# Running sums turned to rows by TensorE, new buffer rule and new order in a scheduled attention and two-MLP kernel

## The chip, the cores and the metric

The kernel runs on 1 core of a Trainium2 chip. Its time is device microseconds of one execution; the runs before the change took 653.19 to 654.08 us, median 653.97 us of 3. Besides, one execution was recorded by the hardware profiler. Engines: PE is TensorE's matmul, PEld its weight load, DVE is VectorE, ACT ScalarE, POOL GpSimd, SP SyncE, which here issues all loads and stores.

## The reference

Attention for 4 batches of 8 heads, 576 tokens, head width 64, with a bias from running sums of s; then two MLP blocks over all 2304 tokens. Cut to what matters:

```python
scores = q @ k.T / sqrt(64)
cum = cumsum(maximum(s, 0), axis=-1)
bias = -(cum[:, None] - cum[None, :])            # per head
scores = where(causal, -1e9, scores + minimum(bias, 0))
attn = softmax(scores)                           # sum + 1e-9
x = (attn @ v)                                   # heads side by side: 2304 x 512
h = x @ w_in; e = exp(h - max(h)); u = h * e / sum(e)
ln = (u - mean(u)) / sqrt(var(u) + 1e-6) * g_ln  # 1024 wide
x2 = ln @ w_out                                  # back to 512
out = maximum(maximum(x2 @ w1, x2 @ w2), x2 @ w3) @ w_out2
```

## The kernel before

**Work.** Two batches form a pair p (c = 0, 1 names the batch in it). A pair has nine tiles t of 128 tokens: for j = 0 to 3 one tile of each batch, and a last one with the 64 left-over tokens of both. Per tile: `prep` loads k, q and v and turns k and q (for the first tiles by TensorE, `turned`, later by a transposing DMA), `scores` multiplies, `half` masks, exponentiates and turns the result, `values` multiplies with v, `m1` does the first MLP's input side. Tiles go two by two into nine groups; per group `m2` multiplies with w_out, `m3` with w1, w2, w3 and takes the maxima (L1257), `m4` with w_out2. Nearly all values are split into a high and a low 16-bit part, and each product is three matmuls of parts.

**Weights.** Each of 40 weight pieces of 512 columns arrives as a 64-bit pattern in one of four staging buffers (the second halves of `kt` and `vs`, not yet needed) and is decoded by `load_w`: three VectorE instructions (L654, L660, L663), a ScalarE copy to the high part (L668), and the low part either by TensorE and ScalarE (L672, L675) or by one more VectorE instruction (L678).

**The bias.** The running sums `cum` of s are put into the scores by a product of their own (L854): `ckr` holds for each head three 16-bit parts of the sums beside rows of ones, `cq` the same for the queries. Batch c and the head's parity y own rows 32c + 64y up. `prologue` computes the sums with heads on partitions (L578 relu, L580 scan, L589 and L588 split in three), writes them to DRAM as `cum_d` (L591), and `load_c` and `load_cq` read them back turned into rows (L603, L616). The first tile's scores need ckr and cq of its pair.

**The order.** `build` writes each operation down with its possible engines, an estimated length and a position `pos`; `Schedule.run` plans them with those estimates: at each step an engine takes among the operations that could start soon (`look`) the one with the smallest pos plus its unit's entry in `off`. The result fixes the order on each engine and the buffer that each operation gets; the semaphores follow from it. The numbers in `P` thus set the order. After the plan is written, an engine works its list in order and waits where an operand is not there. Some loads are held back by hand (L1313 and L1319: the loads of k for tile 1, of v for tile 0, of g and of some weights are issued after the sums' loads).

## Time and profile before

| | |
|---|---|
| median of 3 runs | 653.97 us (653.19 to 654.08) |
| profiled execution | 653.85 us, its span 652.1 us |
| busy: PE, DVE, ACT, POOL | 608.0, 451.4, 328.4, 5.1 us |
| HBM read | 35.95 MB |

The span runs from the first to the last instruction of the program; what the execution takes beside it lies around it. Busy time is the union of an engine's instructions; matmuls overlap, so a busy TensorE is not at its peak. A wait names the engine or DMA whose event came last.

### The profile page before, as it was taken

The numbers are of one execution on the slowest core, as the hardware profiler recorded it, in microseconds if no ns is written. First come the engines' busy times: TensorE is split into PE (matmuls) and PEld (weight loads), VectorE is DVE, ScalarE is ACT, GpSimd is POOL, SyncE is SP. The second block draws the span as 40 slices with busy tenths as digits, with TensorE's granted clock in tenths as the row PEclk, the third lists the DMA queues.
The fourth block names the chain that finished last, engine by engine and source line by source line (L and its number), as shares of the span: only waits on it lengthen the run. The fifth ranks groups of instructions, "written<-read, shape, count | busy, mean of one in ns | idle before, by whom it ended". The sixth has DMA issues, their size and how long they took to land.

```text
span 652.1 us, 15319 instructions
## 1 busy us (share of the span) xinstructions
PE 608.0 (93%) x6203; PEld 447.2 (69%) x6203; DVE 451.4 (69%) x1083; ACT 328.4 (50%) x767; POOL 5.1 (1%) x18
## 2 busy tenths in 40 slices
PE   3386888899999999999999999999999999999997
PEld 1154546785777778778687678677777777777884
DVE  7489999999598659663878676585858576526031
ACT  4378987358565547563644444473446455303100
POOL 3000000000000000000000000000000000000000
PEclk9999899999999999999999999999999999999999
DMA  6579675687999657838769685765374456421001
GB/s 174 172 224 250 169 183 171 193 155 135 180 142 169 146 118 124 150 52 174 123 121 185 134 166 94 131 121 91 73 137 92 93 89 106 82 50 33 33 1 32
DMA packets 249830, 82.67 MB, mean 127 GB/s; under 512 B 226048, under 2 KB 244576, under 8 KB 249760
## 3 DMA queue, kind: packets, MB, share of 16 engines
q1 hardware_dynamic: 249760, 81.70, 61.5%
q8 instruction: 48, 0.79, 0.5%
q14 instruction: 22, 0.18, 0.1%
HBM read 35.95 MB, written 4.83 MB: 63 GB/s over the span
## 4 chain that ended last, share of the span: by engine, by line
PE 81%; DVE 11%; DMA 3%; issue 2%; ACT 2%; SPq 1%; DVEq 0%
PE acc L1238 31%; PE acc L1199 13%; PE w L1102 12%; PE acc L1272 11%; PE w L860 4%; PE av L1029 3%; DVE acc L660 3%; PE w L854 2%; DVE acc L663 2%; PE av L1016 2%; PE acc L486 1%; DVE f L654 1%; DVE w_h L678 1%; DMA kt<-in_moe_w_in_dram 1%; DMA et<-es 1%
## 5 line engine op out<-in xcount | busy, mean ns | idle before, releaser
L1238 PE MATMUL acc<-x2A,w_h 128*128 128x256 f16 x1296 | 214.4, 273 | 2.2 <-DVE f L1257 1.5
L1238 PEld LDWEIGHTS <-w_h 128*128 128x128 f16 x1944 | 188.0, 98 | 27.8 <-issue 4.0
L1238 PE MATMUL acc<-x2B,w_h 128*128 128x256 f16 x648 | 176.8, 273 | 0.0
L945 ACT ACTIVATE r<-r,mn 128x128 f32<-128x128 f32 (+4 forms) x144 | 83.0, 578 | 52.2 <-DVE mn L892 42.0
L1102 PE MATMUL w<-w_in_h,xt 128*128 128x512 f16 x432 | 100.2, 381 | 0.3 <-ACT xt L503 0.3
L1199 PE MATMUL acc<-lnt,w_out_h 128*128 128x256 f16 x864 | 98.6, 273 | 0.4 <-ACT lnt L503 0.4
L1199 PEld LDWEIGHTS <-w_out_h 128*128 128x128 f16 x864 | 83.4, 98 | 13.3 <-issue 1.5
L446 DVE SCALAR_TENSOR_TENSOR es<-r,es 128x512 f16<-128x512 f32 (+1 forms) x92 | 58.2, 638 | 24.0 <-ACT es L417 23.8
L1102 PEld LDWEIGHTS <-xt 128*128 128x128 f16 x432 | 41.6, 98 | 47.4 <-issue 2.6
L1257 DVE TENSOR_TENSOR f<-f,acc 128x512 f32<-128x512 f32 x54 | 37.0, 686 | 45.6 <-PE acc L1238 45.3
L892 DVE CUSTOM_DVE_ANT_0 r<-w,mask 128x128 f32<-128x128 f32 (+3 forms) x128 | 58.3, 487 | 9.8 <-PE w L860 8.4
L1272 PE MATMUL acc<-w2o_h,h2A 128*128 128x512 f16 x216 | 64.5, 380 | 0.0
L417 ACT ACTIVATE es<-r 128x512 f16<-128x512 f32 (+1 forms) x73 | 42.8, 592 | 40.5 <-DMA et<-es 34.8
L466 ACT ACTIVATE f<-acc 128x512 f32<-128x512 f32 x37 | 22.0, 595 | 81.7 <-PE acc L1238 49.7
L860 PE MATMUL w<-kt,qt 64*128 64x256 f16 (+2 forms) x768 | 45.0, 262 | 0.0
L1116 DVE TENSOR_SCALAR_CACHE_REDUCE e<-w 128x1024 f32<-128x1024 f32 x18 | 22.0, 1223 | 31.7 <-PE w L1102 31.7
L1029 PEld LDWEIGHTS <-et 128*128 128x128 f16 x960 | 35.0, 99 | 9.8 <-issue 2.6
L1272 PE MATMUL acc<-w2o_h,h2B 128*128 128x512 f16 x108 | 41.0, 380 | 0.0
L1029 PE MATMUL av<-vs,et 128*128 128x64 f16 x960 | 37.6, 195 | 1.1 <-ACT et L503 0.6
L860 PEld LDWEIGHTS <-qt 64*128 64x128 f16 (+1 forms) x864 | 33.9, 102 | 5.8 <-issue 1.3
L854 PE MATMUL w<-ckr,cq 64*128 64x128 bf16 (+5 forms) x192 | 25.7, 308 | 12.0 <-DMA ckr<-cum_d 11.2
L1272 PEld LDWEIGHTS <-h2A 128*128 128x128 f16 x216 | 19.5, 98 | 21.1 <-issue 2.0
(132 smaller groups left out, 688.4 us busy)
## 6 DMA issues: line engine op xcount, KB each, us to landing
kt<-in_moe_w_dram SPq DMA_DIRECT2D x18, 256.0 KB
vs<-in_moe_w_dram SPq DMA_DIRECT2D x18, 256.0 KB
raw<-in_k_dram SPq DMA_DIRECT2D x16, 256.0 KB
raw<-in_q_dram SPq DMA_DIRECT2D x16, 256.0 KB
raw<-in_v_dram SPq DMA_DIRECT2D x16, 256.0 KB
out_dram<-f SPq DMA_DIRECT2D x16, 256.0 KB
kt<-in_moe_w_out_dram SPq DMA_DIRECT2D x7, 512.0 KB
vs<-in_moe_w_out_dram SPq DMA_DIRECT2D x7, 512.0 KB
```

The costliest lines, as they stand in the source:

```text
L417: eng.activation(out=out(g), in_=src(g), func=AF.Copy, scale=sc(g))
L446: nc.vector.scalar_tensor_tensor(out=lo(g), in0=src(g), scalar=sc1(g), in1=hi(g), op0=ALU.mult, op1=ALU.subtract)
L854: yield lambda: nc.tensor.matmul(out=out(), lhsT=T["cq"][i][r, hp, 0:ts.stop - ts.start], rhs=T["ckr"][r, hp, ck], start=True, stop=False, ...
L860: yield lambda n=n, qa=qa, o=o, kx=kx: nc.tensor.matmul(out=out()[:, o], lhsT=qv()[r, qa * HP + hp, ts], rhs=kx, start=False, stop=(n == 2 ...
L892: nc.vector.tensor_tensor_reduce(out=gw(R)[:, g], in0=gw(sc[y])[:, g], in1=T["mask"][:, SM - W:SM], scale=1.0 / S_MUL, scalar=3e38, op0=AL ...
L945: nc.scalar.activation(out=gw()[:, g], in_=gw()[:, g], func=AF.Exp, bias=mnf()[:, g:g + 1], scale=-1.0, accum_out=den(hs[g]),)
L1029: nc.tensor.matmul(out=out, lhsT=ea_[:, ea, kb], rhs=T["v_s"][c, kb // 2][:, kb % 2, ha + a, va], start=(kb == 0 and m == 0), stop=(kb == ...
L1102: nc.tensor.matmul(out=hb()[:, n * 512:(n + 1) * 512], lhsT=xt()[:, xa, kk], rhs=T["w_in_h"][:, wa, kk, n * 512:(n + 1) * 512], start=(kk ...
L1199: nc.tensor.matmul(out=ps()[:, d % 2 * GN:(d % 2 + 1) * GN], lhsT=T["w_out_h"][:, wa, kk, d * 128:(d + 1) * 128], rhs=lnt()[:, la, kk], st ...
L1238: nc.tensor.matmul(out=ps()[:, f % 2 * GN:(f % 2 + 1) * GN], lhsT=T["w123_h"][:, w, wa, f, kk], rhs=x2(xa)[:, kk], start=(kk == 0 and i == ...
L1257: op([("DVE", dve2(2 * GN), lambda ps=ps: nc.vector.tensor_tensor(out=m(), in0=m(), in1=ps(), op=ALU.max))], pk + [m], [m], pos, kind="m3x")
L1272: nc.tensor.matmul(out=ps(), lhsT=h2(ha)[:, f, o * 128:(o + 1) * 128], rhs=T["w2o_h"][:, wa, f], start=(f == 0 and i == 0), stop=(f == KF2 ...
```

## The change

The sums are computed in two pieces, columns 0 to 127 first (relu, scan, split), then the rest. `first_sums` multiplies the first piece with `pick`, a matrix of zeros and ones that sends heads to the rows of ckr and cq, 24 matmuls in two buffers of PSUM; ScalarE or VectorE copies the results to ckr's first 128 columns and to cq, with signs and ones from `rows`. The sums still go to DRAM; ckr's other 448 columns, and cq from tile 2 on, come from there. The scores of tiles over 128 columns wait for the second key `ckB`. For batch 0 the bias product reads 33 rows, not 64, and does not wait for batch 1's. g is loaded as 8 rows of 128 and turned by one matmul. The loads held back by hand behind the sums' loads are no longer so.

The planner's rules: an operation whose buffer another has begun is planned no earlier than that buffer's release (`since`), no more than eight transfers are open at once, and estimates of some lengths differ. P's numbers, `off` with several hundred entries above all, set another order on every engine.

```diff
--- before.py
+++ after.py
...
-    la=5.521,
...
+    la=-6.043,
...
-    off={},
+    off={
+        "c": -52.41, "c.": -55.92, "c0.": -56.71, "c1.": -57.46, "h0.0": -17.18, "h0.2": -32.17,
...
+                    at = max(at, b.since)
...
+                lanes = lanes[1:] + [o.end]
+                free[e] = max(free[e], lanes[0])
...
+                    h = b.pool.holder[b.slot]
+                    b.since = h.end + self.LAT_CROSS if h else 0
...
+    def first_sums(c3, cb, pos):
+        for n in range(2):
+            wb = buf("w")
+            def f(n=n, wb=wb):
+                for x in range(HP):
+                    for i in range(3):
+                        m = 3 * n + 3 - i
+                        nc.tensor.matmul(
+                            out=wb()[:, x * 128:(x + 1) * 128], lhsT=T["pick"][0:BH, x, m:m + 128], rhs=c3()[:, i, 0:128],
+                            start=(i == 0), stop=(i == 2), skip_group_check=True,
+                        )
+            op([("PE", pe(12, 128) + 100, f)], [(cb, 0), "pick"], [wb], pos + n, kind="cs")
+            ps = lambda wb=wb: wb()[:, 0:HP * 128].rearrange("p (x t) -> p x t", t=128)
+            for c in range(2) if n else (None,):
+                def f_a(c=c, ps=ps):
+                    nc.scalar.activation(
+                        out=T["ckr"][:, :, 0:128] if c is None else T["cq"][c], in_=ps(), func=AF.Identity,
+                        scale=1.0 if c is None else T["rows"][:, c:c + 1], bias=T["rows"][:, 2 if c is None else 3 + c:][:, 0:1])
+                def f_v(c=c, ps=ps):
+                    if c is None:
+                        nc.vector.tensor_scalar(out=T["ckr"][:, :, 0:128], in0=ps(), scalar1=T["rows"][:, 2:3], scalar2=None, op0=ALU.add)
+                    else:
+                        nc.vector.tensor_scalar(
+                            out=T["cq"][c], in0=ps(), scalar1=T["rows"][:, c:c + 1], scalar2=T["rows"][:, 3 + c:4 + c],
+                            op0=ALU.mult, op1=ALU.add)
+                op([("ACT", act(512, True, False, True), f_a), ("DVE", dve2(512) + 61, f_v)], [wb, "rows"],
+                   [("ck", x, y) for x in range(2) for y in range(2)] if c is None else [("cq", c, y) for y in range(2)],
+                   pos + n + (c or 0) / 4, kind="ce")
...
-            op([("POOL", 400, lambda c=c: nc.gpsimd.memset(T["cq"][c].bitcast(F32), 0.0))],
-               [], [("cq", c, y) for y in range(2)], p0, kind="one")
...
+        op([("POOL", 330, lambda: nc.gpsimd.memset(T["pick"], 0.0))], [], ["pick"], p0 - 0.9, kind="one")
+        op([("DVE", 90, lambda: nc.vector.tensor_copy(
+            T["pick"][:, :, 6:6 + 128].rearrange("p x (y c r) -> p x y c r", y=2, c=2)[:, :, :, :, 0],
+            IDENT()[0:BH, 0:2 * H].rearrange("p (c x y) -> p x y c", c=2, y=2)))], ["ktail", "pick"], ["pick"], p0 - 0.9, kind="one")
...
+        for n, (lo, hi) in enumerate(((0, 128), (128, S))):
+            w = hi - lo
+            op([("ACT", act(w) + 60, lambda lo=lo, hi=hi: nc.scalar.activation(
+                out=spt()[:, lo:hi], in_=spt()[:, lo:hi], func=AF.Relu, scale=S_MUL))],
+               [sp], [(sp, n)], p0 + n / 2, kind="relu0")
+            def scan(lo=lo, hi=hi):
+                nc.vector.tensor_tensor_scan(
+                    out=cmt()[:, lo:hi], data0=spt()[:, lo:hi], data1=spt()[:, lo:hi],
+                    initial=cmt()[:, lo - 1:lo] if lo else 0.0, op0=ALU.add, op1=ALU.max)
+            op([("DVE", w * 1.71 + 300, scan)], [(sp, n)] + [(cum, 0)] * n, [(cum, n)], p0 + n / 2, kind="scan")
+            def parts(lo=lo, hi=hi):
+                sl, cl = spt()[:, lo:hi], cmt()[:, lo:hi]
+                for i in range(3):
+                    src = cl if i == 0 else sl
+                    if i:
+                        nc.vector.tensor_tensor(out=sl, in0=cl if i == 1 else sl, in1=c3()[:, i - 1, lo:hi], op=ALU.subtract)
+                    nc.vector.tensor_copy(c3()[:, i, lo:hi], src)
+            op([("DVE", 2450 if n else 1900, parts)], [(cum, n), (sp, n)], [(sp, n), (cb, n)], p0 + n / 2 + 0.1, kind="c3")
+            if n == 0:
+                first_sums(c3, cb, p0 + 0.2)
...
+                op([("SP", 450, lambda c=c, y=y, r0=r0: nc.sync.dma_start(out=T["ckr"][r0:r0 + 3, :, lo:S], in_=cd[2 * p + c, y][:, :, lo:S]))],
+                   ["cum_d", "ck1"], [("ck", c, y)] * (p > 0) + [("ckB", c, y)], pos, dma=300, kind="c")
+            if p:
+                load_cq(t + c, pos)
...
-            out=T["g_sb"], in_=X["g_ln"].rearrange("(k p) -> p k", p=128), single_packet=False))],
-            [], ["g0"], P["wo"] - 0.5, dma=448, kind="g")
+            out=T["g_raw"], in_=X["g_ln"].rearrange("(k p) -> k p", p=128)))],
+            [], ["g0"], P["wo"] - 0.5, dma=30, kind="g")
+        gp = buf("w")
+        op([("PE", 200, lambda: nc.tensor.matmul(
+            out=gp()[:, 0:KF], lhsT=T["g_raw"], rhs=IDENT()[0:KF, 0:KF], is_transpose=True, start=True, stop=True,
+            skip_group_check=True))], ["g0", "ktail", "prime"], [gp], P["wo"] - 0.5, kind="gp")
         op([("DVE", 73, lambda: nc.vector.tensor_scalar(
-            out=T["g_sb"], in0=T["g_sb"], scalar1=W_S, scalar2=None, op0=ALU.mult))], ["g0"], ["g"], P["wo"] - 0.5, kind="gs")
+            out=T["g_sb"], in0=gp()[:, 0:KF], scalar1=W_S, scalar2=None, op0=ALU.mult))], [gp], ["g"], P["wo"] - 0.5, kind="gs")
...
-        keyed = [(x, i, y) for x in ("ck", "cq") for i in ((0, 1) if tail else (c,)) for y in range(2)]
+        both = (0, 1) if tail or c else (0,)
+        keyed = [("cq", i, y) for i in ((0, 1) if tail else (c,)) for y in range(2)] + [
+            (x, i, y) for x in ("ck", "ckB")[:1 + (W > 128)] for i in both for y in range(2)]
...
+            rb = slice(64 * y, 64 * y + (64 if i else 33))
-                out=out(), lhsT=T["cq"][i][r, hp, 0:ts.stop - ts.start], rhs=T["ckr"][r, hp, ck], start=True, stop=False,
+                out=out(), lhsT=T["cq"][i][rb, hp, 0:ts.stop - ts.start], rhs=T["ckr"][rb, hp, ck], start=True, stop=False,
...
-    for k, n in (("ldk1", "cum"), ("ldv0", "c00"), ("ldq1", "c00"), ("g", "c00")):
-        named[k].after.add(named[n])
...
```

TensorE, first scores. The order of before from the copies of q on (`qt` is q's transposed tile, `acc` and `w` are buffers in PSUM):

```order
L500 MATMUL acc_130<-qt_89,k_tail 128x512
L672 LDWEIGHTS k_tail
L672 MATMUL acc_131<-w_in_h,k_tail 128x512
L672 LDWEIGHTS k_tail
L672 MATMUL acc_129<-w_in_h,k_tail 128x512
L854 LDWEIGHTS cq_79
L854 MATMUL w_126<-ckr,cq_79 128x128
```

The same place after (`lnt_112` holds the split sums):

```order
L591 MATMUL acc_133<-qt_92,k_tail 128x512
L628 LDWEIGHTS pick
L628 MATMUL w_130<-lnt_112,pick 128x128
...
L628 MATMUL w_129<-lnt_112,pick 128x128
L1008 LDWEIGHTS cq_79
L1008 MATMUL w_130<-ckr,cq_79 128x128
```

Two weight products (L672) stood ahead of the first scores; now the 24 products with pick stand there, and no weight product.

VectorE, from the split of the sums to the first mask-add (ISA with `mask`), before (`f` holds a decoded half, `kt` and `vs` are the staging buffers):

```order
L589 CAST lnt_109<-ln_108 32x576
L654 TENSOR_SCALAR f_115<-kt_69 128x512
...
L663 SCALAR_TENSOR_TENSOR acc_130<-kt_69,acc_130 128x512
L654 TENSOR_SCALAR f_115<-vs_73 128x512
L660 SCALAR_TENSOR_TENSOR acc_131<-vs_73,f_115 128x512
L663 SCALAR_TENSOR_TENSOR acc_131<-vs_73,acc_131 128x512
L697 TENSOR_SCALAR g_sb<-g_sb 128x8
L892 ISA r_91,mn_118<-w_126,mask 128x128
```

And after:

```order
L733 CAST lnt_112<-ln_111 32x448
L801 TENSOR_SCALAR f_118<-kt_69 128x512
L801 TENSOR_SCALAR f_119<-vs_73 128x512
L807 SCALAR_TENSOR_TENSOR acc_134<-kt_69,f_118 128x512
L807 SCALAR_TENSOR_TENSOR acc_132<-vs_73,f_119 128x512
L810 SCALAR_TENSOR_TENSOR acc_134<-kt_69,acc_134 128x512
L810 SCALAR_TENSOR_TENSOR acc_132<-vs_73,acc_132 128x512
L801 TENSOR_SCALAR f_120<-kt_71 128x512
L1046 ISA r_94,mn_121<-w_130,mask 128x128
```

Four pieces are decoded ahead of the first mask-add before, two pieces and the first step of a third now.

VectorE, last decode and group 1's `x2B` (the low part of m2's result), before:

```order
L663 SCALAR_TENSOR_TENSOR acc_131<-vs_75,acc_131 128x512
L446 SCALAR_TENSOR_TENSOR es_94<-r_92,es_94 128x384
L1128 ISA e_107,st_125<-e_107,ln_108 128x1024
...
L446 SCALAR_TENSOR_TENSOR xs_106<-f_116,xs_106 128x512
L1216 SCALAR_TENSOR_TENSOR x2B_112<-acc_129,x2A_111 128x512
```

And after:

```order
L1370 SCALAR_TENSOR_TENSOR x2B_115<-acc_132,x2A_114 128x512
L1046 ISA r_96,mn_123<-w_130,mask 128x384
...
L825 SCALAR_TENSOR_TENSOR w2o_h<-acc_134,w2o_h 128x512
L801 TENSOR_SCALAR f_119<-vs_75 128x512
L807 SCALAR_TENSOR_TENSOR acc_132<-vs_75,f_119 128x512
L537 SCALAR_TENSOR_TENSOR es_97<-r_94,es_97 128x384
L810 SCALAR_TENSOR_TENSOR acc_132<-vs_75,acc_132 128x512
...
L1370 SCALAR_TENSOR_TENSOR x2B_115<-acc_133,x2A_114 128x512
```

Before, group 1's first x2B stands 39 rows behind the last decode (L663). Now it stands ahead of the last decode (L810), and the second x2B seven rows behind that.

## Rows read from the trace of the kernel before

**Rows 1.** The page, busy us, share of the span and instructions.

```profile
PE 608.0 (93%) x6203; PEld 447.2 (69%) x6203; DVE 451.4 (69%) x1083; ACT 328.4 (50%) x767; POOL 5.1 (1%) x18
```

**Rows 2.** The page, the chain that ended last, by engine.

```profile
PE 81%; DVE 11%; DMA 3%; issue 2%; ACT 2%; SPq 1%; DVEq 0%
```

**Rows 3.** Busy time in stretches: length; PE, PEld, DVE, ACT, POOL; PEclk, DMA, GB/s.

```profile
0.00:150.00 150.00, 112.16 (x907) 74.00 (x907) 132.08 (x313) 96.61 (x226) 5.13 (x18) 0.99 0.70 186
150.00:200.00 50.00, 48.85 (x538) 36.16 (x537) 40.47 (x100) 34.45 (x81) 0.00 (x0) 1.00 0.94 160
200.00:500.00 300.00, 300.00 (x3218) 223.31 (x3216) 208.25 (x511) 153.28 (x367) 0.00 (x0) 1.00 0.68 125
...
27.20:151.00 123.80, 105.16 (x875) 70.42 (x874) 119.53 (x291) 89.79 (x217) 0.00 (x0) 0.99 0.70 182
```

**Rows 4.** TensorE's waits over the whole span: us in total, times, longest.

```profile
PE w L854 <- DMA ckr<-cum_d: 11.2, 2, 10.1
```

**Rows 5.** VectorE's waits in the first 30 us, same columns.

```profile
DVE r L892 <- PE w L860: 8.1, 1, 8.1
DVE f L654 <- DMA kt<-in_moe_w_in_dram: 2.7, 2, 1.9
...
DVE f L654 <- DMA vs<-in_moe_w_in_dram: 0.7, 1, 0.7
```

**Rows 6.** SyncE's queue in order of time: start, length in us, what.

```profile
0.80 0.41 SPq L534 DMA_DIRECT2D ln<-in_s_dram  x1
```

**Rows 7.** TensorE in order of time, the first scores.

```profile
25.23 0.26 PE L854 MATMUL w<-ckr,cq 64*128 64x128 bf16 x1 [1.18 <-DMA ckr<-cum_d]
...
25.53 0.39 PE L854 MATMUL w<-ckr,cq 64*128 64x128 bf16 x2
...
25.96 0.39 PE L854 MATMUL w<-ckr,cq 64*128 64x128 bf16 x2
```

**Rows 8.** VectorE in order of time, five places.

```profile
5.42 0.75 DVE L588 TENSOR_TENSOR ln<-e,lnt 32x576 f32<-32x576 f32 x1
...
6.69 0.75 DVE L588 TENSOR_TENSOR ln<-ln,lnt 32x576 f32<-32x576 f32 x1
...
8.64 0.43 DVE L654 TENSOR_SCALAR f<-kt 128x512 int32<-128x512 int32 x1 [0.72 <-DMA kt<-in_moe_w_in_dram]
...
27.25 0.29 DVE L892 CUSTOM_DVE_ANT_0 r<-w,mask 128x128 f32<-128x128 f32 x1 [8.13 <-PE w L860]
...
151.52 0.70 DVE L663 SCALAR_TENSOR_TENSOR acc<-vs,acc 128x512 int32<-128x512 int32 x1
```

**Rows 9.** ScalarE in order of time, two places.

```profile
2.85 0.68 ACT L578 ACTIVATE ln<-ln 32x576 f32<-32x576 f32 x1 [0.77 <-DMA ln<-in_s_dram]
...
8.18 0.60 ACT L503 ACTIVATE qt<-acc 128x512 f16<-128x512 f32 x1 [0.18 <-PE acc L500]
```

**Rows 10.** VectorE by line and shape: busy us, mean ns of one, idle before.

```profile
L663 DVE SCALAR_TENSOR_TENSOR acc<-kt,acc 128x512 int32<-128x512 int32 x20 | 13.8, 690 | 0.2
...
L654 DVE TENSOR_SCALAR f<-kt 128x512 int32<-128x512 int32 x20 | 8.3, 417 | 2.7 <-DMA kt<-in_moe_w_in_dram 2.7
...
L580 DVE TENSOR_TENSOR_SCAN e<-ln 32x576 f32<-32x576 f32 x1 | 1.3, 1345 | 0.3 <-ACT ln L578 0.3
...
L589 DVE CAST lnt<-ln 32x576 bf16<-32x576 f32 x2 | 0.9, 447 | 0.1
```

**Rows 11.** SyncE's queue, the last issues.

```profile
648.15 1.18 SPq L1285 DMA_DIRECT2D out_dram<-f  x2
```

**Rows 12.** POOL in order of time, two places.

```profile
1.08 0.65 POOL L542 TENSOR_SCALAR_AFFINE_SELECT k_tail<-k_tail 128x128 f32<-128x128 f32 x2
...
5.03 1.25 POOL L574 TENSOR_SCALAR_AFFINE_SELECT maskt<-maskt 64x64 bf16<-64x64 bf16 x2
```

**Rows 13.** TensorE by line and shape, two groups of 256 columns.

```profile
L1238 PE MATMUL acc<-x2A,w_h 128*128 128x256 f16 x1296 | 214.4, 273 | 2.2 <-DVE f L1257 1.5 <-ACT f L466 0.7
...
L860 PE MATMUL w<-kt,qt 64*128 64x256 f16 x384 | 30.1, 269 | 0.0
```

More of the change, by code (lines that the diff above doesn't have):

```diff
@@ L577, in prologue @@
         op([("POOL", 500, tri)], ["maskt"], ["maskt"], p0, kind="mask")
-        op([("ACT", 640, lambda: nc.scalar.activation(out=spt(), in_=spt(), func=AF.Relu, scale=S_MUL))],
-           [sp], [sp], p0, kind="relu0")
-        op([("DVE", 669, lambda: nc.vector.tensor_tensor_scan(
-            out=cmt(), data0=spt(), data1=spt(), initial=0.0, op0=ALU.add, op1=ALU.max))],
-            [sp], [cum], p0, kind="scan")
-        def parts():
-            for i in range(3):
-                src = cmt if i == 0 else spt
-                if i:
-                    nc.vector.tensor_tensor(out=spt(), in0=cmt() if i == 1 else spt(), in1=c3()[:, i - 1], op=ALU.subtract)
-                nc.vector.tensor_copy(c3()[:, i], src())
@@ L590, in prologue @@
-        op([("DVE", 3 * dve1(S) + 2 * dve2(S) + 300, parts)], [cum, sp], [sp] + [(cb, i) for i in range(3)], p0 + 0.5, kind="c3")
-        named["cum"] = op([("SP", 450, lambda: nc.sync.dma_start(out=T["cum_d"], in_=c3()))], [(cb, i) for i in range(3)], ["cum_d"],
+        for n, (lo, hi) in enumerate(((0, 128), (128, S))):
[18 more added lines that the diff above has]
+                first_sums(c3, cb, p0 + 0.2)
@@ L592, in prologue @@
+        named["cum"] = op([("SP", 450, lambda: nc.sync.dma_start(out=T["cum_d"], in_=c3()))], [(cb, 0), (cb, 1)], ["cum_d"],
            p0 + 3, dma=205, kind="cum_d")
@@ L598, in load_c @@
         t = p * (2 * NB + 1)
+        lo = 0 if p else 128
         for c in range(2):
@@ L1311, in build @@
                 m4(g, o)
-    for k, n in (("ldk1", "cum"), ("ldv0", "c00"), ("ldq1", "c00"), ("g", "c00")):
-        named[k].after.add(named[n])
     for k, n in enumerate(P["wa"]):
-        if n in named:
-            for i in range(2):
-                if ("w", k, i) in named:
-                    named["w", k, i].after.add(named[n])
+        for i in range(2):
+            if ("w", k, i) in named:
+                named["w", k, i].after.add(named[n])
     return S_, pools
```

96 lines of the change are left out of this document (53 added, 43 removed), and 84 rows, old and new, of the table off.

## The prediction

> **What bounds the kernel now.** I read the page's busy shares first [rows 1]: TensorE is busy 93% of the 652.1 us span. That number is an average over stages with different limits, so the next view is the chain that ended last [rows 2]: 81% of it is TensorE, but 11% (some 72 us) is VectorE. The stretches say where [rows 3]: from 200 to 500 us TensorE is busy 300.00 of 300 us; in the first 150 us it is busy only 112.16, so nearly all of its idle time (37.8 of 44 us) lies there. In 27.2 to 151 us VectorE is busy 119.53 of 123.80 us. The kernel is thus a VectorE-bound start followed by a TensorE-bound rest, and what the change is worth is how much sooner the start is over.
>
> Why does the VectorE stretch begin only at 27 us? TensorE's waits [rows 4] hold one large entry: 11.2 us, 10.1 of it at once, for the load of ckr from cum_d, the running sums that went to DRAM and back. VectorE's waits [rows 5] show the same hole from its side: 8.1 us for the first scores, and 3.4 us in three waits (2.7 of them for one stage) for the first weights. The timelines give the instants: s is asked for at 0.80 [rows 6], the scores run from 25.23 [rows 7], the first mask-add starts at 27.25 [rows 8].
>
> **The first scores, new chain.** The load of g now stands ahead of s, so s and all behind it go out one issue later, 0.41 us by the issue of s [rows 6]. The relu, at 2.85 us before [rows 9], starts at 3.3 and is done at 3.7. VectorE meanwhile writes the constants: the six new small instructions (pick and rows) have no row; the nearest, a cast of 576 columns, took 447 ns [rows 10], so 2.7 us at most, and by columns (64 of 576) 0.3 at least; they are nearer to the small end but wait for one another, so I take 1.0. They follow the minus block, and are over at about 4.2. The scan took 1345 ns for 576 columns [rows 10]; in two pieces I take 1.6 us, bounds 1.35 to 1.9. Copying g out, 0.2, comes between. The five splitting instructions took 3 x 0.45 [rows 10] and 2 x 0.75 us [rows 8] for 576 columns, 2.8 us; the first 128 columns cost at least 128/576 of that, 0.6, at most all of it; I take 1.2. The first sums are ready at 4.2 + 1.6 + 0.2 + 1.2 = 7.2 us. TensorE is then still turning k and q (q's last copy began at 8.18 before [rows 9]; 8.6 with the later loads). The 24 new matmuls of 128 columns: at the scores' pace, eight from 25.53 to 25.96 and two at a time [rows 7], 0.05 us each, 1.3 us; one alone took 0.26 [rows 7], 6.2 us. They don't wait for one another but go one at a time, so I take 0.107 each, 2.6. Copying out to ckr and cq: ckr overlaps the second twelve, then one ACT copy like L503's 0.60 us [rows 9], and a handover. First score: 8.6 + 2.6 + 0.8 = 12.0 us, bounds 10.5 to 16, against 25.2. POOL drops six memsets, adds one, and is done earlier than now.
>
> The product over 33 instead of 64 rows I cost at nothing (bounds: nothing either way): over 256 columns a product of 128 rows took 273 ns and one of 64 rows 269 [rows 13], so rows are not what it pays for. What it changes is who is waited for: c = 0 no longer needs rows 32 up. SyncE issues four cq loads less. On its queue cum_d now stands behind v of tile 0 and k of tile 1, which wait until TensorE has turned the first k and q (7 to 8 us); ckr's other columns come later for it by 1 or 2 us, but are needed only from tile 2 on.
>
> **VectorE in front of the first mask-add.** Before, four weight pieces are decoded there, after only two and the first step of a third: the order rows show it. The second splitting block (448 columns, 2.2 us by the same rows) ends at 9.5; the two weights land at 9 and 11 (the first decode began at 8.64 [rows 8], behind a wait); two decodes of 0.42 + 2 x 0.69 us [rows 10] end at 14.2 with about 1 us of waiting. The scores, 2.0 us from 25.23 to 27.2 now [rows 7, 8], are ready at 14.0. So the first mask-add starts at 14.5 instead of 27.25, but two decodes (3.2 us net of the first step) are still owed.
>
> **The VectorE stretch.** From the first mask-add to the 40th and last decode VectorE takes 27.25 to 152.2, 125 us, with 4 us idle [rows 3, 8]. Counted in the order, the same stretch has two decodes and a multiplication more and some conversions less after the change: +3.2 us. Last decode: 14.5 + 125 + 3.2 = 142.7. Two us later stands x2B's last piece for group 1, and behind it group 1's first L1238 product at about 145.
>
> What has TensorE done by then? The order has 1069 matmuls ahead of that product, 25 of them new, so 1044 of the old ones. In the trace of before 907 are done at 150 us and 538 more in the next 50 [rows 3]: the 1044th stands at 150 + 137/538 x 50 = 162.7 us. If TensorE is at VectorE's heels at this place, the rest starts 162.7 - 145 = 17.7 us sooner, the 25 new matmuls included. For small stalls of TensorE's own I take 1.5 us off: 16 us.
>
> **The rest and the end.** Past that point TensorE is full [rows 3] and its work is the same, so nothing is won or lost there in the likeliest case. 46 VectorE instructions less over the whole program, 50 ScalarE ones and 12 pairs on POOL more: VectorE and ScalarE are busy 69% and 51% in 200 to 500 us [rows 3], which covers the exchange; without that cover ScalarE's 50 would cost some 30 us (50 x 0.60 [rows 9]). After the last copy the two output issues take 1.18 us [rows 11]; one is left, at most 0.6 us less, bounds -0.6 to +0.6; I take zero. Sum: 652.1 - 16 = 636.1 us of span; the profiled execution took 1.75 us more than its span (653.85), and the median of the runs, 653.97, is that execution within 0.02%. Forecast 638.0.
>
> **Where a rule speaks against it.** The 12 POOL pairs scale and subtract tiles in SBUF beside a full VectorE. In the trace, a VectorE subtraction with two SBUF inputs took 0.75 us at 5.42 beside POOL's mask work and 0.75 us at 6.69 after it [rows 8, 12]; POOL's two 64-column selects took 1.25 us there, its two 128-column ones 0.65 us earlier [rows 12]. So VectorE was not slowed, POOL was.
> The Trainium skill, SBUF — State Buffer, section "SBUF: two separate sides", says that VectorE (with two SBUF inputs, or in a two-port mode) and GpSimd share one port pair under an exclusive lock: who starts first holds it for the whole instruction and the other blocks fully. By that rule POOL's slowness agrees, but a long POOL instruction that starts first would stop VectorE, which no row of before shows.
>
> **Rivals.**
> 1. Starved start. With four loads issued together and VectorE 13 us ahead, each early decode waits for its load as the first four did, 3.4 us over four [rows 5]; over the next eight that is 6.8 us: 645. For it: 0.70 mean DMA share already [rows 3]. Against: in 30 to 152 us VectorE never waited for a load.
> 2. More is kept. Ahead of the first maximum (L1257) the new order has 29 decodes instead of 33 at the same count of matmuls (663, 667). The four decodes and four low parts (4 x 2.5 us by [rows 10]) and some 2.3 us of conversions (four, of L654's and L663's widths) are off VectorE by then; with the 12.7 - 3.2 from above it comes 22 us earlier. If TensorE holds that lead: 653.85 - 22 = 632. Against: the decodes come back at once.
> 3. Slower: POOL stops VectorE. The 24 instructions on 512 columns have no row; between one 128-column select, 0.33 us, and four times that [rows 12], they take 8 to 31 us. If all stop VectorE for their whole length, net of 12 subtractions of 0.69 (L663's width [rows 10]) that it no longer does, 0 to 23 us; at the upper end, with the chain of q and k behind each pair (2.6 us instead of 0.7) holding TensorE too, 638 + 23 = 661. It decides once more than 16 us of this falls where VectorE is full. Against: five of the pairs stand ahead of 145 us by the order, at most 13 us.
> 4. It doesn't do what it says: the first scores wait for another late part, as the second half of the sums or tile 1's q, and the order gives back what is left: 653 to 655.
>
> **Chances.** Forecast 0.60, its own range 634 to 643; rival 1 0.18; rival 2 0.12; rival 3 0.05; rival 4 0.05. The range 630 to 649 holds the first three; it leaves out rivals 3 and 4 and the outer ends. About 0.2% (1.3 us) is what can be told from no change. Faster 0.60 + 0.18 + 0.12 + 0.02 = 0.92; same 0.03; slower 0.05.
>
> **What would show it.** Right: the first L1008 product (L854 before) at 10.5 to 16 us with no wait for DRAM, the first mask-add near 14.5, VectorE without a gap over 2 us until the last decode at about 143, TensorE idle in the first 150 us down from 38 to about 23, nothing new idle after 200. Wrong: VectorE waiting for loads in 15 to 60 us (rival 1), VectorE's 128x512 subtractions longer than 0.68 us beside POOL (rival 3), or TensorE idle past 200 us.

## The result and the profile after

The changed kernel takes 644.35 us, the median of four executions (640.97 to 645.13), against 654.03 us before (653.19 to 654.57) on the same chip: a ratio, worked out from all the executions and not from the two medians, of 0.9843, with an interval of 0.9807 to 0.988. Five more executions of it beside the first experiments gave 643.37 us. So it is 9.7 to 11 us faster, where 16 were forecast; the time lies 6.35 us above the forecast, inside the range of 630 to 649, but 1.35 us outside the forecast's own 634 to 643. The profiled execution is the fastest of the nine: 640.97 us, with a span of 639.3.

The page, busy time and, below, the chain that ended last by engine [rows 1, 2]:

```profile
PE 608.3 (95%) x6228; PEld 448.5 (70%) x6228; DVE 427.5 (67%) x1041; ACT 356.7 (56%) x817; POOL 26.0 (4%) x37
...
PE 68%; DVE 14%; DMA 11%; ACT 3%; issue 2%; SPq 1%; DVEq 0%; ACTq 0%
```

TensorE is as busy as before and idle 31.0 instead of 44.1 us. ScalarE has 28.3 us more to do, VectorE 23.9 less, POOL 20.9 more. In the chain VectorE's share did not fall; DMA's rose from 3% to 11%. Followed piece by piece, these 71 us are 47 us of DMA transposes and 24 us of loads. The longest single piece is a load in the start, of v of tile 0, which landed at 14.24 us:

```profile
6.16 8.08 DMA raw<-in_v_dram
```

The starting phase, TensorE and then VectorE in order of time [rows 7, 8]:

```profile
8.33 1.58 PE L628 MATMUL w<-lnt,pick 32*128 32x128 bf16 x24
10.78 0.23 PE L1008 MATMUL w<-ckr,cq 33*128 33x128 bf16 x2 [0.87 <-ACT cq L636]
...
4.45 0.16 DVE L699 SCALAR_TENSOR_TENSOR rows<-rows 128x1 f32<-128x1 f32 x1
4.53 0.41 DVE L722 TENSOR_TENSOR_SCAN e<-ln 32x128 f32<-32x128 f32 x1
5.05 1.14 DVE L722 TENSOR_TENSOR_SCAN e<-ln,e 32x448 f32<-32x448 f32 x1
6.12 0.13 DVE L848 TENSOR_SCALAR g_sb<-w 128x8 f32<-128x8 f32 x1
6.18 0.20 DVE L733 CAST lnt<-e 32x128 bf16<-32x128 f32 x1
...
7.44 0.38 DVE L733 CAST lnt<-e 32x448 bf16<-32x448 f32 x1
...
13.57 0.28 DVE L1046 CUSTOM_DVE_ANT_0 r<-w,mask 128x128 f32<-128x128 f32 x1
...
144.79 0.70 DVE L810 SCALAR_TENSOR_TENSOR acc<-vs,acc 128x512 int32<-128x512 int32 x1
```

The bracket behind the first score names ScalarE's copy to cq, not a load: the trip through DRAM is gone. The first mask-add has no bracket: VectorE came to it without waiting.

Next, one execution of each kernel cut into three stretches at which TensorE has the same work behind it: I added the columns of all products but the 25 new ones in order of time, and cut where 21% and where 61% of them are done. A product of 64 rows or fewer counts half and one of 64 rows and 64 output rows a quarter, because TensorE's steps from product to product show two and four of them at a time (0.059 and 0.032 us on average for 256 columns past 200 us in before, against 0.110 for 128 rows). Columns as in [rows 3]; first before, then after:

```profile
0.00:189.00 189.00, 150.02 (x1321) 100.78 (x1323) 161.65 (x387) 122.53 (x289) 5.13 (x18) 0.99 0.75 180
189.00:423.30 234.30, 234.30 (x2530) 176.72 (x2530) 165.30 (x412) 123.40 (x294) 0.00 (x0) 1.00 0.73 135
423.30:652.10 228.80, 223.66 (x2355) 169.68 (x2353) 124.40 (x285) 82.49 (x186) 0.00 (x0) 1.00 0.40 74
```

```profile
0.00:172.00 172.00, 149.03 (x1338) 102.97 (x1339) 155.90 (x383) 125.14 (x291) 3.09 (x13) 0.94 0.76 190
172.00:412.00 240.00, 236.97 (x2673) 174.51 (x2671) 181.79 (x458) 157.81 (x376) 22.94 (x24) 1.00 0.86 152
412.00:639.30 227.30, 222.34 (x2222) 171.00 (x2219) 89.80 (x202) 73.76 (x152) 0.00 (x0) 1.00 0.30 59
```

The first stretch is 17.0 us shorter: what was forecast. The middle one is 5.7 us longer for the same work of TensorE: what was not. There ScalarE is busy 157.81 instead of 123.40 us, VectorE 181.79 instead of 165.30, the DMA engines 0.86 instead of 0.73. Most of this comes forward from the last stretch, where VectorE has 34.6 us less, ScalarE 8.7, and the DMA engines 0.30 instead of 0.40; in the first stretch VectorE has only 5.8 us less and ScalarE 2.6 more. TensorE's products say the same: of the 1408 products with v, 740 lie in the middle stretch now, before 596; 126 of these 144 were in the last stretch before, 18 in the first. The new order does more of the attention in the middle and more of the MLPs at both ends. The last stretch is 1.5 us shorter.

TensorE's waits in the middle stretch of after (before has one there, of 0.3 us):

```profile
PE av L1183 <- DMA et<-es: 1.0, 3, 0.6
PE w L1008 <- DVE mn L1046: 0.9, 1, 0.9
PE w L1256 <- DMA xt<-xs: 0.6, 1, 0.6
PE acc L1353 <- DMA lnt<-ln: 0.4, 1, 0.4
```

Five of the six waits are for DMA transposes of what VectorE and ScalarE have just written. The six make 2.9 us, which is the idle time of that stretch (240.0 - 236.97 = 3.0). The other 2.7 us lie inside TensorE's busy time (236.97 against 234.30 for the same work), because a product's modelled end covers the first part of a wait. Taken from the start of a product to the start of the next, less the usual step of its shape (0.109 us for 256 columns), the six steps with these waits lose 4.0 us; in the second trace (e1 below) seven such steps lose 4.8 us, in before and in e5 there is none over 0.22 us. The rest, some 1.5 us, goes with the mix of products: more short ones with v, and five more changes from scores to other products at 0.13 us each. The last stretch has fewer of both.

### The profile page after: what moved, and what is told of

Read it like the earlier page. It is cut to its first block, busy times and chain, and to the rows that moved or that the text cites. A ratio compares the mean times of both kernels' runs of the same rounds, so it can differ in the third digit from the quotient of the medians.

```text
span 639.3 us, 15430 instructions
## 1 busy us (share of the span) xinstructions
PE 608.3 (95%) x6228; PEld 448.5 (70%) x6228; DVE 427.5 (67%) x1041; ACT 356.7 (56%) x817; POOL 26.0 (4%) x37
## 4 chain that ended last, share of the span: by engine, by line
PE 68%; DVE 14%; DMA 11%; ACT 3%; issue 2%; SPq 1%; DVEq 0%; ACTq 0%
PE acc L1392 27%; PE acc L1353 13%; PE w L1256 10%; PE acc L1426 8%; DMA et<-es 4%; PE av L1183 3%; PE w L1014 2%; DVE r L1046 2%; DMA raw<-in_v_dram 2%; DVE acc L807 2%; PE av L1170 2%; DVE acc L810 2%; PE acc L577 1%; PE w L1008 1%; DMA lnt<-ln 1%
## 5 line engine op out<-in xcount | busy, mean ns | idle before, releaser
L1099 ACT ACTIVATE r<-r,mn 128x512 f32<-128x512 f32 (+4 forms) x144 | 82.8, 577 | 29.3 <-DVE mn L1046 17.8
L1353 PE MATMUL acc<-lnt,w_out_h 128*128 128x256 f16 x864 | 96.1, 273 | 1.6 <-ACT lnt L594 0.8
L537 DVE SCALAR_TENSOR_TENSOR es<-r,es 128x512 f16<-128x512 f32 (+1 forms) x92 | 59.5, 651 | 20.1 <-ACT es L508 19.5
L508 ACT ACTIVATE es<-r 128x512 f16<-128x512 f32 (+1 forms) x77 | 44.4, 584 | 27.5 <-DMA et<-es 26.9
L557 ACT ACTIVATE f<-acc 128x512 f32<-128x512 f32 x41 | 24.2, 590 | 55.2 <-PE acc L1392 31.3
L1014 PE MATMUL w<-kt,qt 64*128 64x256 f16 (+2 forms) x768 | 43.3, 256 | 0.0
L1277 ACT ACTIVATE ln<-e,st 128x1024 f32<-128x1024 f32 x18 | 20.7, 1149 | 28.5 <-DVE e L1270 22.6
L1014 PEld LDWEIGHTS <-qt 64*128 64x128 f16 (+1 forms) x864 | 32.4, 98 | 4.7
```

The costliest lines, as they stand in the source:

```text
L508: eng.activation(out=out(g), in_=src(g), func=AF.Copy, scale=sc(g))
L537: nc.vector.scalar_tensor_tensor(out=lo(g), in0=src(g), scalar=sc1(g), in1=hi(g), op0=ALU.mult, op1=ALU.subtract)
L557: nc.scalar.activation(out=out(*a), in_=in_(*a), func=AF.Copy, scale=scale)
L1014: yield lambda n=n, qa=qa, o=o, kx=kx: nc.tensor.matmul(out=out()[:, o], lhsT=qv()[r, qa * HP + hp, ts], rhs=kx, start=False, stop=(n == 2 ...
L1099: nc.scalar.activation(out=gw()[:, g], in_=gw()[:, g], func=AF.Exp, bias=mnf()[:, g:g + 1], scale=-1.0, accum_out=den(hs[g]),)
L1353: nc.tensor.matmul(out=ps()[:, d % 2 * GN:(d % 2 + 1) * GN], lhsT=T["w_out_h"][:, wa, kk, d * 128:(d + 1) * 128], rhs=lnt()[:, la, kk], st ...
```

## The experiments

Each was timed in its own rounds beside the kernel before, which took 654.46, 654.26 and 654.22 us in the three groups of four; ratios are to that. The three numbers behind each kernel are its stretches in us, cut as above.

| kernel | us | ratio, interval | first | middle | last |
|---|---|---|---|---|---|
| before | 654.03 | | 189.0 | 234.4 | 228.8 |
| after | 644.35 | 0.9843, 0.9807 to 0.988 | 171.9 | 239.8 | 227.5 |
| e1 after again | 643.37 | 0.9844, 0.9823 to 0.9865 | 174.1 | 240.6 | 226.8 |
| e2 old numbers | 662.22 | 1.0124, 1.0105 to 1.0142 | 187.4 | 243.1 | 229.8 |
| e3 sums through DRAM | 649.38 | 0.9929, 0.9904 to 0.9954 | 180.2 | 243.6 | 226.4 |
| e4 no POOL pairs | 643.62 | 0.9841, 0.9815 to 0.9867 | 171.8 | 240.7 | 227.1 |
| e5 chain alone | 645.18 | 0.9857, 0.9841 to 0.9874 | 180.5 | 234.2 | 228.7 |
| e6 VectorE more | 650.18 | 0.9935, 0.9918 to 0.9952 | 179.3 | 241.4 | 226.8 |
| e7 TensorE more | 646.93 | 0.9886, 0.9868 to 0.9905 | 176.2 | 241.3 | 227.2 |
| e8 late loads out | 641.19 | 0.9794, 0.9771 to 0.9818 | 172.7 | 238.7 | 227.8 |
| e9 loads by POOL | 652.2 | 0.9967, 0.9944 to 0.9989 | 175.2 | 247.7 | 227.8 |
| e10 small edits undone | 645.73 | 0.9862, 0.984 to 0.9885 | 174.8 | 241.2 | 228.0 |
| e11 ScalarE more | 648.9 | 0.9915, 0.9888 to 0.9943 | 173.5 | 243.8 | 226.3 |
| e12 chain moved up | 645.57 | 0.987, 0.9852 to 0.9887 | 180.6 | 235.0 | 228.9 |

**e1, the changed kernel again** (no edit).

> The changed kernel once more, nothing edited, for a second trace of it and as the measure for the runs beside it. Its four executions lay between 640.97 and 645.13 us (before: 653.19 to 654.57). In the first trace TensorE is 17.0 us ahead of before when the stage bound by VectorE is over (at 172 us), and keeps only 11.9 us of it at 412 us, by some eight waits for late DMA transposes and one for a maximum. Theory, late transposes: the second trace is again 16 to 17.5 us ahead at 172 us, the waits past that point add up to another number (3 to 8 us), and the time follows them, 640.5 to 645.5. Rival, half clock in the start: the lead at 172 us itself differs by 2 us or more, as the granted clock of the first 60 us does, and the waits past it add up to the same 5 us.

The second trace loses 6.2 us in the middle (5.4 in the first, by the table), and its first stretch is 2.2 us longer. So the loss in the middle comes again, and neither theory was right about the scatter: most of it arises in the first stretch. The mean granted clock does not explain it. It is 0.94 there in the first trace and 0.95 in the second, which is the slower one, and 0.98 in e8 (172.7 us). The loads of the first 40 us go with it. ScalarE's wait for v of tile 0, then VectorE at the first instruction that waits for ScalarE's work behind it, and once more further on, in the first trace:

```profile
ACT vs L508 <- DMA raw<-in_v_dram: 2.9, 1, 2.9
...
18.39 0.70 DVE L807 SCALAR_TENSOR_TENSOR acc<-kt,f 128x512 int32<-128x512 int32 x1 [1.50 <-ACT w_in_h L822]
...
44.66 0.68 DVE L1217 TENSOR_TENSOR f<-av,den 128x512 f32<-128x512 f32 x1
```

The same in the second, with one more late load between:

```profile
ACT vs L508 <- DMA raw<-in_v_dram: 4.2, 1, 4.2
...
19.43 0.70 DVE L807 SCALAR_TENSOR_TENSOR acc<-kt,f 128x512 int32<-128x512 int32 x1 [1.12 <-ACT w_in_h L822]
...
32.79 0.43 DVE L801 TENSOR_SCALAR f<-kt 128x512 int32<-128x512 int32 x1 [0.71 <-DMA kt<-in_moe_w_out_dram]
...
46.66 0.68 DVE L1217 TENSOR_TENSOR f<-av,den 128x512 f32<-128x512 f32 x1
```

VectorE is 1.0 us later behind v, and 2.0 us later by 44.66, nearly the whole 2.2. That these loads are the cause is argued from two traces, not tried.

**e2, the new code with the planner's numbers of before.**

```
-P = dict(la=-6.043, ..., look=[0.0, 125.3, ...], off={...})
+P = dict(la=5.521, ..., look=[142.7, 33.8, ...], off={})
```

> The new code (first sums by TensorE, 33 rows, g by rows, planner rules) with the planner's numbers of before (la to look, spare, no off table; the early weights keep waiting for q's first load only). Theory, the new chain carries the gain: the first score is at 10.5 to 12 us and VectorE is busy from then on, so 641 to 648 us. Rival, the new order carries it: an early first score with the old order gives VectorE back what it won, 651 to 655 us. Both halves: 647 to 651.

662.22 us, slower than before and past both theories, although the first score stands at 10.69. The early first score alone assures nothing: the numbers and the planner's rules go together, and this mixture makes an order of its own. Its first stretch is only 1.6 us shorter than before's, its middle one 8.7 and its last 1.0 us longer. It is no measure of the chain; e5 is.

**e3, the new order with the sums through DRAM.**

```
-nc.tensor.matmul(out=wb()[:, ...], lhsT=T["pick"][0:BH, x, m:m + 128], rhs=c3()[:, i, 0:128], ...)
+nc.sync.dma_start(out=T["cum_d"][:, :, 0:128], in_=c3()[:, :, 0:128])
-nc.scalar.activation(out=T["ckr"][:, :, 0:128] if c is None else T["cq"][c], in_=ps(), ...)
+nc.sync.dma_start(out=T["ckr"][r0:r0 + 3, :, 0:128], in_=cd[i, y][:, :, 0:128])
```

> The new order on every engine, instruction for instruction, with one thing undone: the first 128 columns of the split sums go to DRAM and come back to ckr and cq by eight small loads (one store and eight loads more on SyncE's queue, between k of tile 1 and the rest of the sums; no pick products, no rows constants; POOL writes cq's constants again). The split is over at 7.4 us; the store and the loads each take about 2 us and up to nine issues of 0.5 us, behind 1.1 MB of loads already asked for: first score at 15 to 21 us instead of 10.8. Theory, each us that the first scores come later is a us at the end: 649 to 655 us. Rival, the order carries the gain, because it has other VectorE work to do in that hole: 643 to 647 us.

649.38 us. TensorE's first score in this kernel:

```profile
18.34 0.60 PE L1006 MATMUL w<-ckr,cq 33*128 33x128 bf16 x2 [9.96 <-DMA cq<-cum_d]
```

It comes 7.6 us later than in after, and the end comes 6.0 us later: the first theory, at its lower edge. Still the kernel is 5 us faster than before. That is not the order's worth alone: the sums are still made in two pieces, and come back by small loads, so that the first score is 6.9 us earlier than before's 25.23. The trace is of one of the slower executions (651.9 us).

**e4, no POOL pairs.**

```
+if o.eng == "POOL" and o.kind[-1] == "l":
+    o.fn = next(x[2] for x in o.alts if x[0] == "DVE")
```

> The new order, with the twelve scale-and-subtract pairs of POOL (between 194 and 362 us, 22.9 us busy) put back to VectorE as twelve subtractions of 0.69 us, 8.3 us more, at the same places. In the first trace VectorE's instructions with both inputs in SBUF lasted longer beside POOL's (868, 1361, 881 and 2059 ns instead of 687 and about 1215), some 4.5 us in all. Theory, TensorE is the bound there and VectorE has room: within 1 us of the changed kernel either way. Rival A, the stopped VectorE is what makes TensorE wait past 172 us: 2 to 4 us faster. Rival B, VectorE has no room for 8.3 us more: 2 to 4 us slower.

643.62 us against 643.37: no difference, the theory. The pairs together cost nothing and give nothing that can be told from nothing. The middle stretch is as long without them. VectorE is busy there 184.55 instead of 181.92 us (e1): part of the 8.3 us that it got back replaces the time in which POOL stopped it, so the two rivals could also cancel in part.

**e5, the chain alone in the old order.**

```
+if o.kind == "Pq" and first:
+    sched.first_sums()
...
-op([("SP", 450, lambda ...: nc.sync.dma_start(out=T["ckr"][r0:r0 + 3], ...
+op([("SP", 450, lambda ...: nc.sync.dma_start(out=T["ckr"][r0:r0 + 3, :, lo:S], ...
```

> The kernel before, its order kept on every engine, with only the new way of the first 128 columns: 24 pick products on TensorE right behind q's low part, three ScalarE copies to ckr and cq, the constants for them on VectorE behind the minus block; the loads of ckr bring columns 128 up, the first cq loads are gone; nothing else is taken over (one scan, one split of 576 columns, 64 rows, g as before, no POOL pairs). The first scores then stand behind the second weight's low part and can start at about 13.7 us instead of 25.2; VectorE's first mask-add stands behind four decodes and comes at 19 to 21 us instead of 27.25. Theory, the start bound by VectorE is what the change shortens: 6 to 8 us, 646 to 648.5 us. Rival 1, the new code with the old numbers lost 8 us because the new chain doesn't fit an old order (loads of weights and tokens that come out of step): 653 us or more. Rival 2, the whole gain in an old order: 641 to 645 us.

645.18 us, 9.1 faster than before, a little more than the theory gave: most of the whole gain without the new order. The first score stands at 15.92, the first mask-add at 19.5. The stretches show what the order adds: e5 has 180.5 and 234.2, after 171.9 and 239.8. The new order wins 8.6 us more in the start and gives 5.6 back in the middle; by e1's trace it wins 6.4 and gives 6.4 back. By the times, what it adds to the chain alone (0.6 to 2 us) is not told apart from nothing: the intervals of e5, e1 and after overlap.

The times do not add: 9.1 us for the chain alone, 5.1 for e3, 11.1 for both (e1). The first stretches nearly do: 8.5 us shorter in e5, 8.8 in e3, 17.1 in after and 14.9 in e1. The two shorten it in different ways, as VectorE's busy time (third number behind the length) shows, first e5, then e3:

```profile
0.00:30.00 30.00, 15.80 (x92) 8.12 (x93) 23.58 (x67) 17.91 (x41) 5.80 (x19) 0.67 0.76 221
0.00:180.50 180.50, 151.62 (x1345) 102.20 (x1345) 162.45 (x397) 124.78 (x292) 5.80 (x19) 0.91 0.78 189
```

```profile
0.00:30.00 30.00, 14.81 (x89) 8.84 (x90) 19.33 (x56) 14.53 (x37) 4.62 (x18) 1.00 0.70 182
0.00:180.20 180.20, 148.34 (x1314) 101.97 (x1315) 155.08 (x373) 122.81 (x288) 4.62 (x18) 0.98 0.74 182
```

The chain takes idle time out of the first 30 us (before 13.7, e5 6.4, e3 10.7 us idle); the new order takes work out of the stretch (before 161.65, e5 162.45, e3 155.08). What spoils the sum is the middle, which e3 too loses in.

**e6 and e7, more work for one engine in the start.** First VectorE, then TensorE:

```
+if o.kind == "dec1":
+    n += 1
+    if 9 <= n <= 26:
+        o.fn()
```

> The changed kernel, its order kept, with the first step of the decodes 9 to 26 (a shift of 128x512, 0.42 us, about 30 to 95 us into the span) executed twice: 18 x 0.42 = 7.6 us more on VectorE in the starting stretch, the same results. Theory, VectorE sets the end of that stretch: 5.5 to 8 us longer, 649 to 651.5 us. Rival, TensorE or the loads set it: at most 2 us, 643.4 to 645.5 us.

```
+if o.kind == "m1" and o.again and o.unit in ("m0", "m1", "m2"):
+    o.again()
+    o.again()
```

> The changed kernel, its order kept, with 36 matmuls of 128x512 more (three for each half of the first product of tiles 0, 1 and 2, twice, overwritten by the real ones; 28 to 70 us into the span): 36 x 0.216 = 7.8 us more on TensorE in the starting stretch at the full clock, the same results. Theory, VectorE sets the end of that stretch and TensorE has some 23 us idle there: 0 to 3 us longer, 643.4 to 646.5 us. Rival, TensorE at its granted clock is as much the bound: 6 to 8 us longer, 649.5 to 651.5 us.

Against e1, 7.6 us of VectorE make the kernel 6.8 us longer, 90% of it; 7.8 us of TensorE make it 3.6 us longer, 46% (the theory had 0 to 3). VectorE sets the end of the start in the main. TensorE is close behind it and hides only half of such an addition, although it has 23 us idle there: idle time is of use only where it falls together with the added work. ScalarE was not tested in the start. It is busy 33.7 of the 35 us from 45 to 80 in after, as much as VectorE (33.9), and VectorE's longest waits in the first stretch are for it; its part there stays open.

**e8, the late loads left out**, on top of e4's edit.

```
+if o.kind[:2] == "ld" and int(o.cls.split("@")[1]) > 8:
+    continue
```

> As the run without POOL pairs (643.6 us), and without the loads of q, k and v of tiles 9 to 17 (27 x 256 KB in packets of 256 bytes, some 130 to 480 us into the span): those tiles compute on what the buffers held, so the output is not the reference's. Between 172 and 412 us the new order lets TensorE lose 5.5 to 6.3 us against before, most of it in waits for DMA transposes (es to et, x) and for maxima. Theory A, the transposes are late because they share the queues with these loads: most of it comes back, 638 to 641 us. Theory B, they are late because VectorE and ScalarE have es and x ready late in the new order: within 1 us, 642.6 to 644.6 us.

641.19 us, 2.4 less than e4, 0.2 us outside theory A and with intervals that just touch; the middle stretch is 2.0 us shorter. The loads have a part in the late transposes, about a third of the loss, and not most of it.

**e9, the late loads asked for by GpSimd**, on top of e4's edit.

```
+if o.kind[:2] == "ld" and int(o.cls.split("@")[1]) > 8:
+    sched.queue[0] = nc.gpsimd
```

> As the run without POOL pairs (643.6 us), with the loads of q, k and v of tiles 9 to 17 asked for by GpSimd instead of SyncE; the bytes and packets are the same. Leaving these loads out gave 641.2 us. Theory A1, they cost because each takes some 0.55 us of SyncE's queue ahead of a transpose: 640.5 to 642.3 us. Theory A2, they cost by the time that their packets take on the DMA engines: 642.8 to 645 us. Rival, asking from GpSimd is itself dearer (it writes the descriptors and disturbs VectorE, or starts the loads at another time): 646 us or more.

652.2 us, the rival: 8.6 us dearer. TensorE's longest group of waits in its middle stretch:

```profile
PE av L1183 <- DMA et<-es: 5.4, 8, 2.4
```

The transposes come later still. SyncE's queue was therefore not shown to be what holds them.

**e10, the small edits undone.**

```
-rb = slice(64 * y, 64 * y + (64 if i else 33))
+rb = r
...
-out=T["g_raw"], in_=X["g_ln"].rearrange("(k p) -> k p", p=128)
+out=T["g_sb"], in_=X["g_ln"].rearrange("(k p) -> p k", p=128), single_packet=False
```

> The changed kernel and its order, with the first bias product over 64 rows again (33 before this edit) and g loaded by columns as before (8 words for each of 128 partitions, still ahead of s on SyncE's queue, no product for it). By the trace a pair of 33-row products of 256 columns takes 109 ns against 110 for 64 rows, so the rows are worth nothing. Theory: 642.5 to 645 us, all of it g's 1024 packets ahead of s (first score at most 1 us later). Rival, the 33 rows let early products start without waiting for rows 32 up: first score or later ones wait, 645.5 to 648 us.

645.73 us, 2.4 more than e1 with intervals that overlap: not told apart from nothing. What there may be lies in the first stretch (174.8), where e1 has 174.1 and after 171.9. There g's load by columns shows in the trace: the relu starts at 4.17 instead of 3.13 us.

**e11, more work for ScalarE in the middle.**

```
+if o.eng == "ACT" and o.kind in ("kh", "qh", "vh", "xh", "eh", "lnh"):
+    n += 165e3 <= o.start and o.start < 400e3
+    if 165e3 <= o.start < 400e3 and n % 3 == 1:
+        o.fn()
```

> The changed kernel and its order, with 31 of ScalarE's scaling copies between about 165 and 400 us (most of them es from r in front of a transpose, and k, q, v, x) executed twice: about 31 x 0.58 = 18 us more on ScalarE, which is busy 170 of the 262 us from 150 to 412, the same results. Theory, what TensorE loses past 172 us (5.5 to 6.3 us) comes from ScalarE's and VectorE's work that the new order put off into that stretch, so that es and x are ready late: 4 to 12 us longer, 647.5 to 655.5 us. Rival, ScalarE has room there and the transposes are late for the queues' sake: at most 2 us longer, 643 to 645.5 us.

648.9 us, 5.5 more than e1, in the theory's range; its executions scatter most (645.29 to 651.73). The profiled one is the fastest of them, with a middle stretch of 243.8 us and these waits in it:

```profile
PE w L1008 <- DVE mn L1046: 4.4, 3, 2.3
PE w L1256 <- DMA xt<-xs: 1.4, 1, 1.4
```

In the new order part of 18 us more of ScalarE, about a third, reaches TensorE. Two things were not tried: the same 18 us in the old order, and as much more work for VectorE in the middle, whose busy time e4 raised by only 2.6 us.

**e12, the chain alone, moved up.**

```
+if n == 3:              # ahead of the third dec1
+    early[1].fn()
+    early[2].fn()
...
 sched.first_sums()
+early[0].fn()
```

> The kernel before with the new chain alone (645.2 us), and in its order two pieces moved: the first group of scores stands on TensorE right behind the pick products, ahead of the first two weights' low parts (first score at 11 to 12 us instead of 15.9), and the eight mask-adds of these scores (1.7 us) stand on VectorE ahead of the third decode, which waited 1.8 us for its load (14.9 us). Theory, VectorE sets the end of the start and this fills its hole: 1.2 to 2 us shorter, 643.2 to 644 us. Rival, the start is then bound by what comes behind (TensorE's low parts, ScalarE's conversions): no change, 644.9 to 646 us.

645.57 us, no change: the rival's number, though not its reason. VectorE in order of time:

```profile
11.78 0.70 DVE L701 SCALAR_TENSOR_TENSOR acc<-vs,acc 128x512 int32<-128x512 int32 x1
15.05 0.29 DVE L930 CUSTOM_DVE_ANT_0 r<-w,mask 128x128 f32<-128x128 f32 x1 [2.57 <-PE w L898]
```

The first mask-add is 4.5 us earlier than in e5 and nothing is won: VectorE now waits 2.57 us for the scores where it waited 1.8 us for the load. In the first 30 us it is busy 23.63 us here and 23.58 in e5. The instant of the first mask-add moved by 4.5 us without effect; the idle time did not move, and neither did the end.

No version here beats the changed kernel; e8 is faster only because it leaves work out.

## Why the prediction was right, and where it was not

**The chain of the first scores: right.** Constants over at 4.6 (4.2 forecast), scans 1.55 (1.6), first split 1.3 (1.2), sums ready at 7.5 (7.2), the picks from 8.33 (8.6). They took 1.58 us here, not 2.6; but in e6, e7, e8, e10 and e11 the same 24 products took 2.74, as in e7:

```profile
8.47 2.74 PE L628 MATMUL w<-lnt,pick 32*128 32x128 bf16 x24
```

The first score stands at 10.78, between the bounds 10.5 and 16 and below the 12.0 chosen, which those five traces met (11.99 to 12.50); the first mask-add at 13.57 (14.5).

**33 rows: right.** The bias product over 256 columns of 64 rows and of 33 rows in after, mean ns last but one [rows 13]:

```profile
L1008 PE MATMUL w<-ckr,cq 64*128 64x256 bf16 x16 | 2.2, 274 | 0.0
L1008 PE MATMUL w<-ckr,cq 33*128 33x256 bf16 x16 | 2.2, 273 | 0.0
```

**The VectorE stretch: right in what bounds it, 3.7 us too short in size.** e6 confirms the bound. From the first mask-add to the last decode it took 131.9 us, not 128.2, so the last decode ends at 145.5 instead of 142.7. Yet TensorE comes to group 1's first product at 146.7 (145 forecast) and has the 1044 old products behind it at 146.8, 15.4 us sooner than before (162.2), where 16 were forecast. Its idle time in the first 150 us fell from 37.8 to 22.9 us, where about 23 were forecast.

The step's arithmetic was weaker than its result. It carried the first mask-add's 12.7 us forward and took 3.2 off; e12 shows that such an instant can move by 4.5 us without effect. VectorE's idle time in the first 30 us is the better measure: 13.7 us before (10.32 and 5.98 busy in the two halves), 6.4 in e5, 4.7 in after, which is busy as this row says:

```profile
0.00:30.00 30.00, 20.38 (x164) 11.94 (x165) 25.31 (x88) 20.69 (x51) 3.09 (x13) 0.77 0.85 233
```

The 7.3 us that e5 wins there stand beside a gain of 9.1. The new order's part of the start (e3) is VectorE work moved behind the cut, 5.4 to 6.6 us; the forecast had it only in its count of the products ahead of group 1.

**"Past that point nothing is won or lost": wrong, and it is the step that failed.** The forecast took ScalarE's 51% and VectorE's 69% busy as cover for the exchange, 50 more ScalarE instructions (28.3 us measured) against less on VectorE. An average share of busy time is no cover when a chain of ScalarE, VectorE and a transpose must be in time for TensorE at each product, and the order put 34.4 of these us and 16.5 of VectorE's into the middle. The middle stretch lost 5.4 to 6.3 us in the two traces of after and in e4, and 0.6 at most in e5 and e12 with the old order: that the order loses it is shown. Of it 4.0 to 5.1 us are TensorE's steps with late operands; the rest is the mix of products. ScalarE's added work (e11) and the loads (e8) move it, so that the cause in the attention brought forward fits, but is argued; VectorE's share was hardly tested (e4). Rival 2 had said that the new order leads by more, and that "the decodes come back at once". It does lead by more, 6.4 to 8.6 us over e5 in the first stretch; what took that back is not the decodes, whose last ends at 145.5, but the middle, 5.6 to 6.4 us.

**The number.** The forecast of 638 missed by about what the middle loses. Rival 1 had named 645, 0.65 us off, for another reason that the traces bear out only in small part (below): its number is luck.

**The tail: 1.0 us shorter, outside the 0.6 taken as bound.** From the end of the last copy to the end of the span it was 3.97 us with two issues [rows 11] and is 2.97 with one:

```profile
636.31 0.34 SPq L1443 DMA_DIRECT2D out_dram<-f  x1
```

Sum for the profiled execution: 17.0 - 5.7 + 1.5 = 12.8 us, as the spans differ. The other executions are 2 to 5 us slower; e1's trace puts 2.2 of that into the first stretch, where two late loads go with it.

**Rival 1, starved start: came only in small part.** In 30 to 160 us VectorE waited 1.0 us for loads (2.0 in e1), not 6.8; TensorE waited 4.6 us for k in two places. But before 30 us ScalarE waited 2.9 us for v of tile 0 (4.2 in e1), and VectorE behind it 1.5.

**Rival 3, POOL stops VectorE: the mechanism is there, the price is not.** All 12 pairs run between 194 and 362 us, none ahead of 145: "five stand ahead by the order" read a position on POOL's queue as a time. They took 0.70 + 1.21 us each, 22.9 in all, inside the bounds 8 to 31. POOL and VectorE in order of time, two places:

```profile
225.66 1.15 POOL L547 TENSOR_TENSOR st<-raw,st 128x512 f16<-128x512 f32 x1
225.80 1.03 DVE L1198 TENSOR_SCALAR den<-den 128x8 f32<-128x8 f32 x1 [0.88 <-ACT r L1099]
...
284.78 1.16 POOL L547 TENSOR_TENSOR vs<-raw,vs 128x512 f16<-128x512 f32 x1
285.12 1.36 DVE L537 SCALAR_TENSOR_TENSOR st<-raw,st 128x512 f16<-128x512 f32 x1
```

A VectorE instruction on 8 columns lasts 1.03 us and ends with POOL's at 226.8; a subtraction of 0.69 us lasts 1.36. So VectorE is stopped, which the rows of before did not show; it comes to some 4.2 us over the 12 pairs, by the usual length of each instruction. The rule of the Trainium skill, SBUF — State Buffer, section "SBUF: two separate sides", that VectorE (in a two-port mode or with two SBUF inputs) and GpSimd lock each other out of a shared port pair, is borne out by these rows. e4 gives the price of the pairs here: none that can be told from nothing.

**Rival 4: refuted** by the first score at 10.78 without a load in its bracket.

## What to carry to other kernels

Where one engine bounds the start, count its idle time and its work in that stretch before and after, and take the instant of its first dependent instruction only as a hint. When a new order moves work from one stretch into another, forwards or back, ask which engine gets it and which transposes hang on it; its average busy share is no answer. Cutting both traces where the bounding engine has the same work behind it shows where a gain is made and where it is lost, and running the old order with the new part alone shows at once what the order is worth. A position in an engine's queue is not a time.
